# The row transposes of two tensors moved from PE to the DMA queue, and those of two others merged, in a fused forward-and-backward kernel

## The chip, the cores and the metric

The kernel runs on one core of one Trainium2 chip. The metric is the device time of one execution in microseconds (us). The time before was 828.26 us (median of 3 runs, 827.59 to 828.33).

The engines are called as the profile calls them: PE is TensorE (matrix multiply), PEld its weight loads, DVE is VectorE, ACT is ScalarE, POOL is GpSimd, SP is SyncE, which here does nothing but issue DMA transfers. "SPq" is SP's queue.

## The reference, cut to what matters

```python
# x [2,16000,256], w1, w2 [3,256,256], g [2,8,256], w_f, w_g, w_o [256,256], all bf16
h  = gelu(conv(x, w1))[:, ::2]          # 3 taps, stride 2
f  = gelu(conv(h, w2))[:, ::2]          # 3 taps, stride 2: 4000 rows per batch
j  = tanh((f @ w_f)[:, :, None] + (g @ w_g)[:, None])
out = j @ w_o                           # [2,4000,8,256]
# returned: out and the gradients of all seven inputs, for a given grad_out
```

The gradient with respect to `h` is what this case is about. The kernel holds it as two tensors, one for the odd rows of `h` (`GHo`) and one for the even rows (`GHe`), each with the 256 channels on partitions (two halves of 128) and time along the free axis. The gradient of `w1` contracts over time, so it needs the same numbers with time on partitions: their row layouts, `GHoR` and `GHeR`.

## The kernel before

The 4000 rows of each batch are cut into chunks of at most 512, 18 chunks in all: 256, seven of 512, 160; seven of 512, 256, 160. The kernel first records operations with modelled costs. A greedy scheduler (`issue`) then fixes the order of each engine's instructions from those costs. In the trace of before, all 6428 matmuls and all 536 DMA instructions of SP start in that order. While chunk k is in its main part (tanh, `j @ w_o`, backward of both), the backward of chunk k-1 (`stage_de`) and the convolutions of chunk k+1 (`stage_a`) fill the gaps.

The row layouts of `GHo` and `GHe` are made on PE, as a multiplication by the identity into PSUM, and copied to SBUF by ACT or DVE:

```python
    def to_rows(cls, SRC, off, n, keys):
        dst = buf(cls, [P, NB, D], BF16, cls.upper())
        ps = psum(BF16)
        nbl = (n + P - 1) // P

        def trs(e):
            for bl in range(nbl):
                m = min(P, n - bl * P)
                for kt in range(KT):
                    nc.tensor.transpose(out=ps[:m, (bl * KT + kt) * P:(bl * KT + kt + 1) * P],
                                        in_=SRC[:, kt, off + bl * P:off + bl * P + m], identity=ident[:])
        op("PE", c_pe([P] * (nbl * KT)), trs, r=[(SRC, k) for k in keys] + [ident], w=[ps], new=[ps, dst])
        # ... one or two evictions ps -> dst by ACT or DVE, cut
```

The rows of `h` itself (`HRo`, `HRs`, `HRe`) and of `f` (`FR`) already come from transposing DMAs that SP issues, one for each half of the channels:

```python
    def dma_rows(name, cls, g_, SRC, off, keys, nb):
        W = chunks[g_][3]
        Wp = (W + P - 1) // P * P
        R = buf(cls, [P, KT, NB, P], BF16, name)
        st[g_][name] = R
        for kt in range(KT):
            dma("SP", lambda kt=kt: R[:, kt, 0:Wp // P, :], lambda kt=kt: SRC[:, kt, off:off + Wp],
                r=[(SRC, kt)] + [(SRC, k) for k in keys], w=[(R, kt)], bytes_=Wp * P * 2, new=[R] if kt == 0 else [],
                transpose=True, nb=nb)
```

What the scheduler believes about a DMA is in these lines. A transposing DMA keeps SP busy for 1260 ns, and its data is counted as there 2000 ns plus a margin of 6500 ns after the modelled transfer:

```python
        c = 1260.0 if transpose else 400.0 if q == "SP" else cost or (750.0 if q == "POOL" else 100.0)
        return op(q, c, go, r=r, w=w, new=new, at=at, after=after, hold=hold, nb=nb,
                  work=bytes_ / 256 * 1.25 if transpose else bytes_ / 300.0)
    # ... in issue():
                o.done = ring[e] + 2000.0 + self.MARGIN          # MARGIN = 6500.0
```

And this is where the rows are made, in `stage_de`, after the weight gradients of the second convolution. They are used last in the stage, after the `gx` matmuls:

```python
        GHoR = to_rows("rows", GHo, 0, Wsp, [0, 1, "z"])
        tick()
        GHeR = to_rows("rows", GHe, 1, Wsp, [0, 1, "z"])
        tick()
        # ... gx: gradient of x from GHo, GHe, W1T; then the three taps of the gradient of w1:
        #     wgrad(ACC1, i, ..., [(X5 rows, GHoR, ...), (X5 rows, GHeR, ...)], out_2[i])
```

## Time and profile before

| what | before |
|---|---|
| median, 3 runs | 828.26 us |
| span of the profiled run | 826.2 us |
| PE / DVE / ACT busy | 97% / 92% / 91% |
| a full chunk repeats every (first weight load of `JT` to that of the next chunk) | 49.20 us |
| time of SP's DMA instructions, summed | 632 us |

The first part of the page gives each engine's busy time, its share of the span and its instructions:

```profile
PE 798.5 (97%) x6428; PEld 593.9 (72%) x6428; DVE 763.1 (92%) x1731; ACT 749.2 (91%) x1206; POOL 186.6 (23%) x393
```

Three engines above 90% do not say which one bounds the kernel. The table by stretches does. Its columns are the stretch and its length, then busy time (and instructions) of each engine, the granted PE clock, the busy share of the DMA engines and what they moved:

```profile
core 0: us, PE busy (x) PEld busy (x) DVE busy (x) ACT busy (x) POOL busy (x), PEclk, DMA share, GB/s
50.00:100.00 50.00, 47.77 (x353) 32.86 (x351) 49.01 (x109) 49.38 (x80) 12.14 (x24) 1.00 1.05 218
600.00:650.00 50.00, 50.00 (x394) 36.57 (x393) 47.67 (x101) 46.97 (x71) 10.09 (x21) 1.00 0.94 221
```

In mid-kernel PE has no idle time at all, so PE is the limit there. From 50 to 100 us DVE and ACT are nearly as full as they can be, and PE has 2.2 us to spare.

The work that the change takes from PE, and the evictions that go with it, are in the list of groups by form. The columns are the instruction, its operands, their number, then busy time and mean ns of one, then the idle time before them:

```profile
L314 ACT COPY ROWS<-psb 128x1024 bf16<-128x1024 bf16 x42 | 43.5, 1036 | 0.2 <-PE psb L491 0.2
...
L491 PE MATMUL psb<-ident,GHo 128*128 128x128 bf16 x128 | 10.1, 219 | 0.0
L491 PE MATMUL psb<-ident,GHe 128*128 128x128 bf16 x128 | 10.1, 219 | 0.0
```

There are 256 transposes. "219 ns" is the recorded time of one from start to end, not what it costs a full queue: the records overlap, and 253 of the 256 are followed by the next matmul 55 or 56 ns after their start. The `ROWS` evictions here are those of `GHo`, `GHe`, `NGFE` and `GF` together.

The DMA side: the queues that carry the traffic, with packets, MB and the share of the 16 engines' span that the packets took, and two lines of the table of waits (total us, times, longest):

```profile
q1 hardware_dynamic: 314004, 120.54, 70.5%
q0 software_dynamic: 15840, 49.98, 18.6%
```

```profile
DVE g_sq L706 <- DMA out_dram<-g_sq: 9.9, 4, 4.8
...
PE ps L306 <- DMA GOT<-in_grad_out_dram: 2.1, 1, 2.1
```

The packets of these two queues fill 89% of the DMA engines' time, yet PE waited for a load only once after the weights of the start. The waits of DVE on the stores of `g_sq` are in the tail, where the weight gradients are written out through two buffers.

### The profile page before, as it was taken

To read this page: it belongs to the slowest core of one execution; us is meant where nothing else is said; L and a number is where in the kernel's file an instruction comes from. 1 tells how busy PE (TensorE), PEld (TensorE's weight loads), DVE (VectorE), ACT (ScalarE), POOL (GpSimd) and SP (SyncE) were. 2 spreads that over 40 slices of the span, in tenths; PEclk is the share of its full clock that TensorE was granted. 3 is DMA by queue.
4 is the path that set the end of the run, shared out by engine and by line. 5 is a ranking of instruction groups with operands and counts; after the bars stand their busy time and mean duration, and the time that the engine had idled before them with its cause. 6 is when DMAs were issued, how large, how long until landed. Compare 5 with 4: busy or idle time off the path is not lost.

```text
span 826.2 us, 18042 instructions
## 1 busy us (share of the span) xinstructions
PE 798.5 (97%) x6428; PEld 593.9 (72%) x6428; DVE 763.1 (92%) x1731; ACT 749.2 (91%) x1206; POOL 186.6 (23%) x393
## 2 busy tenths in 40 slices
PE   7789999999999999999999999999999999999994
PEld 5556677686777868787877677686767768788983
DVE  4999999998989999998979999999989999998982
ACT  6999999999898989998899999999998989998752
POOL 3111203122221212232222122122111212213241
PEclk9999999999999999999999999999999999999998
DMA  8979999999899896968799999989899897957442
GB/s 185 238 158 233 220 195 275 239 246 267 190 249 216 205 239 173 250 185 215 163 213 243 221 203 248 202 218 241 192 255 187 225 224 192 245 163 188 122 137 68
DMA packets 330718, 172.06 MB, mean 208 GB/s; under 512 B 275236, under 2 KB 310344, under 8 KB 330628
## 3 DMA queue, kind: packets, MB, share of 16 engines
q1 hardware_dynamic: 314004, 120.54, 70.5%
q0 software_dynamic: 15840, 49.98, 18.6%
q8 instruction: 50, 0.82, 0.5%
q10 hardware_dynamic: 784, 0.39, 0.2%
q14 instruction: 40, 0.33, 0.1%
HBM read 54.44 MB, written 50.34 MB: 127 GB/s over the span
## 4 chain that ended last, share of the span: by engine, by line
PE 75%; DVE 10%; ACT 9%; DMA 3%; issue 2%; DVEq 0%; POOL 0%; ACTq 0%
PE ps L306 61%; PE GWO L306 11%; PE psb L491 4%; DVE NGZ L659 2%; DVE ZS L667 2%; ACT JT L597 2%; ACT g_sq L440 1%; ACT JR L617 1%; ACT JSQ L649 1%; DVE g_s L444 1%; DMA GOT<-in_grad_out_dram 1%; ACT OUT_SB L314 1%; ACT GX_SB L316 1%; DMA XC<-in_x_dram 1%; DMA W<-in_w_dram 1%
## 5 line engine op out<-in xcount | busy, mean ns | idle before, releaser
L597 ACT ACTIVATE JT<-FE,GE 128x512 bf16<-128x512 bf16 (+2 forms) x288 | 188.0, 690 | 0.7 <-DVE FE L319 0.7
L331 POOL DMA_DIRECT2D out_dram<-OUT_SB x136 | 94.9, 698 | 383.6 <-ACT OUT_SB L314 275.0
L659 DVE SCALAR_TENSOR_TENSOR NGZ<-JSQ,ps 128x512 f32<-128x512 bf16 (+2 forms) x252 | 155.0, 618 | 2.3 <-PE ps L306 2.2
L306 PE MATMUL ps<-GOT,WT 128*128 128x512 bf16 (+2 forms) x576 | 153.3, 351 | 2.4 <-DMA GOT<-in_grad_out_dram 2.1
L306 PE MATMUL ps<-WO,JT 128*128 128x256 bf16 x1024 | 154.0, 273 | 1.6 <-ACT JT L597 1.0
L617 ACT ACTIVATE JR<-JR 128x1024 bf16<-128x1024 bf16 x128 | 138.3, 1086 | 4.9 <-DVE JR L610 4.6
L306 PEld LDWEIGHTS <-JT 128*128 128x128 bf16 x1024 | 99.6, 98 | 54.8 <-ACT JT L597 1.8
L314 ACT CAST OUT_SB<-ps 128x512 bf16<-128x512 f32 x205 | 125.9, 615 | 9.5 <-PE ps L306 9.5
L306 PE MATMUL GWO<-GO_R,JR 128*128 128x256 bf16 x1024 | 132.7, 273 | 1.2 <-ACT JR L617 1.2
L667 DVE TENSOR_TENSOR ZS<-ZS,NGZ 128x512 f32<-128x512 f32 (+2 forms) x216 | 133.6, 622 | 0.2
L649 ACT ACTIVATE JSQ<-JT 128x1024 bf16<-128x1024 bf16 (+2 forms) x119 | 117.6, 991 | 12.0 <-DVE NGZ L659 11.9
L306 PEld LDWEIGHTS <-JR 128*128 128x128 bf16 x1028 | 99.9, 98 | 19.4 <-ACT JR L617 2.9
L306 PEld LDWEIGHTS <-WT 128*128 128x128 bf16 x864 | 81.3, 98 | 38.0 <-DMA GOT<-in_grad_out_dram 2.3
L306 PEld LDWEIGHTS <-W 128*128 128x128 bf16 x648 | 61.2, 98 | 56.6 <-DMA W<-in_w_dram 2.8
L306 PE MATMUL ps<-XC,W 128*128 128x512 bf16 (+2 forms) x432 | 92.2, 351 | 0.8 <-DVE NGZ L659 0.8
L306 PE MATMUL ps<-ROWS,X 128*128 128x256 bf16 x768 | 92.0, 273 | 0.0
L610 DVE TENSOR_TENSOR JR<-FER,GEB 128x1024 bf16<-128x1024 bf16 x128 | 88.8, 696 | 1.1 <-PE GWO L306 1.0
L306 PEld LDWEIGHTS <-X 128*128 128x128 bf16 x768 | 75.1, 98 | 9.1
L444 DVE SCALAR_TENSOR_TENSOR g_s<-g_sq,ps 128x512 bf16<-128x512 bf16 (+2 forms) x108 | 66.4, 616 | 14.7 <-ACT HTo L442 11.8
L715 DVE TENSOR_TENSOR ACC<-ACC,ps 128x512 f32<-128x512 f32 x96 | 65.1, 690 | 11.4 <-PE ps L306 11.3
L306 PE MATMUL ps<-WT,GHe 128*128 128x256 bf16 x384 | 73.3, 273 | 0.7 <-ACT ROWS L314 0.7
L306 PE MATMUL ps<-WT,GHo 128*128 128x256 bf16 x384 | 73.1, 273 | 0.7 <-ACT GX_SB L316 0.7
(135 smaller groups left out, 1262.3 us busy)
## 6 DMA issues: line engine op xcount, KB each, us to landing
GO_R<-in_grad_out_dram SPq DMA_DIRECT2D x120, 256.0 KB, 3.9
out_dram<-OUT_SB POOLq DMA_DIRECT2D x120, 256.0 KB, 4.2
X<-in_x_dram SPq DMA_DIRECT2D x60, 320.0 KB, 5.8
out_dram<-GX_SB POOLq DMA_DIRECT2D x60, 256.0 KB, 3.9
GOT<-in_grad_out_dram SPq DMA_TRANSPOSE x144, 3.8
out_dram<-g_sq SPq DMA_DIRECT2D x9, 128.0 KB, 1.9
GO_R<-in_grad_out_dram SPq DMA_DIRECT2D x8, 128.0 KB, 2.7
out_dram<-OUT_SB POOLq DMA_DIRECT2D x8, 128.0 KB, 3.7
```

What stands on the lines that cost most here:

```text
L306: nc.tensor.matmul(ps_ap, lhsT=lhsT, rhs=rhs, start=start, stop=stop)
L314: nc.scalar.copy(out=dst(), in_=src())
L331: return eng_.dma_start(out=out(), in_=in_())
L444: op("DVE", c_dve(W), lambda e, mt=mt, ps=ps: nc.vector.scalar_tensor_tensor(out=s[:, mt, :W], in0=sq[:, mt, :W], scalar=1.0, in1=ps[:, :W ...
L491: nc.tensor.transpose(out=ps[:m, (bl * KT + kt) * P:(bl * KT + kt + 1) * P], in_=SRC[:, kt, off + bl * P:off + bl * P + m], identity=ident[:])
L597: op("ACT", c_act(W, ptr=True), lambda e, j=j, mt=mt: nc.scalar.activation(out=JT[:, j, mt, :W], in_=S["FE"][:, mt, :W], func=ACT.Tanh, bi ...
L610: op("DVE", c_dve(n * 2 * D, 0.5), lambda e, lo=lo, n=n, m=m, JR=JR: nc.vector.tensor_tensor(out=JR[:m, lo % 2:lo % 2 + n], in0=S["FER"][: ...
L617: op("ACT", c_act(n * 2 * D), lambda e, lo=lo, n=n, m=m, JR=JR: nc.scalar.activation(out=JR[:m, lo % 2:lo % 2 + n], in_=JR[:m, lo % 2:lo % ...
L649: nc.scalar.activation(out=JSQ[:, :, :W], in_=JT[:, j, :, :W], func=ACT.Square)
L659: op("DVE", c_dve(W) + 6, lambda e, d2=d2, ps=ps, u=u, zap=zap, JSQ=JSQ: nc.vector.scalar_tensor_tensor(out=zap(), in0=JSQ[:, d2, :W], sca ...
L667: op("DVE", c_dve(W), lambda e, d2=d2, dst=dst, NGZ=NGZ: nc.vector.tensor_tensor(out=dst[:, d2, :W], in0=ZS[:, d2, :W], in1=NGZ[:, :W], op ...
L715: op("DVE", c_dve(512), lambda e: nc.vector.tensor_tensor(out=acc_ap().rearrange("p k d -> p (k d)"), in0=acc_ap().rearrange("p k d -> p ( ...
```

## The change

The intent: take 256 matmuls and half of the `ROWS` evictions off the compute engines by making `GHoR` and `GHeR` with SBUF-to-SBUF transposing DMAs; and, to make room in SP's queue, transpose both halves of the channels in one DMA where the source has no padding columns (`HRe` and `FR` in the 14 full chunks). The core of the diff (the adaptation of the row views in `wgrad` is cut):

```diff
-    def dma_rows(name, cls, g_, SRC, off, keys, nb):
-        W = chunks[g_][3]
-        Wp = (W + P - 1) // P * P
-        R = buf(cls, [P, KT, NB, P], BF16, name)
+    def dma_rows(name, cls, g_, SRC, off, keys, nb=None, at=None):
+
+        n = (chunks[g_][3] + off_extra.get(name, 0) * (chunks[g_][1] == last_ci[chunks[g_][0]]) + P - 1) // P
+        R = buf(cls, [P, KT * NB * P], BF16, name)
 ...
+        if SRC.shape[-1] == n * P:
+            dma("SP", lambda: R[:].rearrange("p (g q) -> p g q", q=P), lambda: SRC[:].rearrange("p k w -> p (k w)"),
+                r=[(SRC, k) for k in [0, 1] + keys], w=[R], bytes_=KT * n * P * P * 2, new=[R], transpose=True, nb=nb, at=at)
+            return R
         for kt in range(KT):
 ...
-        GHoR = to_rows("rows", GHo, 0, Wsp, [0, 1, "z"])
+        GHoR = dma_rows("GHoR", "rows", g_, GHo, 0, ["z"])
         tick()
-        GHeR = to_rows("rows", GHe, 1, Wsp, [0, 1, "z"])
+        GHeR = dma_rows("GHeR", "rows", g_, GHe, 1, ["z"])
```

Note that the merge does not reach the new transposes: `GHo` and `GHe` are 514 columns wide, so `GHoR` and `GHeR` go out as two DMAs each, four a chunk.

More of the change, by code (lines that the diff above doesn't have):

```diff
@@ L253 @@
         start_of.append(start_of[-1] + c[3])
+    off_extra = {"GHoR": 1, "GHeR": 1}
+    last_ci = {c[0]: c[1] for c in chunks}
     nblk = [[(tb, P) for tb in range((W + P - 1) // P)] for (_, _, _, W) in chunks]
@@ L464, in conv_gelu @@
         return go
-    def dma_rows(name, cls, g_, SRC, off, keys, nb):
-        W = chunks[g_][3]
-        Wp = (W + P - 1) // P * P
-        R = buf(cls, [P, KT, NB, P], BF16, name)
+    def dma_rows(name, cls, g_, SRC, off, keys, nb=None, at=None):
+        n = (chunks[g_][3] + off_extra.get(name, 0) * (chunks[g_][1] == last_ci[chunks[g_][0]]) + P - 1) // P
+        R = buf(cls, [P, KT * NB * P], BF16, name)
+        view = lambda: R[:, 0:KT * n * P].rearrange("p (k b q) -> p k b q", k=KT, q=P)
+        R.rows = lambda m, bl: view()[:m, :, bl, :]
+        R.cols = lambda m, bl, d2: view()[:m, d2, bl, :]
         st[g_][name] = R
+        if SRC.shape[-1] == n * P:
+            dma("SP", lambda: R[:].rearrange("p (g q) -> p g q", q=P), lambda: SRC[:].rearrange("p k w -> p (k w)"),
+                r=[(SRC, k) for k in [0, 1] + keys], w=[R], bytes_=KT * n * P * P * 2, new=[R], transpose=True, nb=nb, at=at)
+            return R
         for kt in range(KT):
-            dma("SP", lambda kt=kt: R[:, kt, 0:Wp // P, :], lambda kt=kt: SRC[:, kt, off:off + Wp],
-                r=[(SRC, kt)] + [(SRC, k) for k in keys], w=[(R, kt)], bytes_=Wp * P * 2, new=[R] if kt == 0 else [],
-                transpose=True, nb=nb)
+            dma("SP", lambda kt=kt: view()[:, kt], lambda kt=kt: SRC[:, kt, off:off + n * P],
+                r=[(SRC, k) for k in [kt] + keys], w=[(R, kt)], bytes_=n * P * P * 2, new=[R] if kt == 0 else [],
+                transpose=True, nb=nb, at=at)
+        return R
     def pad_tail(g_, SRC, off):
@@ L483, in to_rows @@
         dst = buf(cls, [P, NB, D], BF16, cls.upper())
+        dst.rows = lambda m, bl: dst[:m, bl, :]
         ps = psum(BF16)
@@ L807, in mms @@
                 for k, (lhs, rhs, bl, m, d2) in enumerate(jobs):
-                    mm(ps[:, d2 * D:(d2 + 1) * D], lhs(bl, m, d2), rhs[:m, bl, :], k == 0, k == len(jobs) - 1)
+                    r_ = rhs.rows(m, bl)
+                    o_ = ps[:, d2 * D:(d2 + 1) * D]
+                    mm(o_ if len(r_.shape) == 2 else o_.rearrange("p (k q) -> p k q", k=KT), lhs(bl, m, d2), r_, k == 0, k == len(jobs) - 1)
             rd = [rhs for _, rhs, _, _ in pairs]
@@ L815, in rows_lhs @@
         def rows_lhs(T_):
-            return lambda bl, m, d2: T_[:m, d2, bl, :]
+            return lambda bl, m, d2: T_.cols(m, bl, d2)
         wgrad(ACCF, 0, lambda: ACCF[:], [(rows_lhs(S["FR"]), NFR, nblk[g_], [S["FR"]])], out_5)
```

## The prediction

> **What bounds the kernel now.** TensorE (PE). The profile page shows PE busy 97% of the 826.2 us span, DVE 92%, ACT 91%. The table of 50 us stretches has PE busy 49.5 to 50.0 of every 50 us from 100 to 800, at clock 1.00. From 75 to 800 us successive matmuls start at the gap of their size (216 ns for 512 columns, 109 for 256, 56 for 128); the excess adds up to about 4 us. So there a matmul that disappears is worth its issue interval, whatever other engines do. Only the first 60 us (loads) and the tail after 802 us (small dependent steps, nine stores through two buffers) are bound otherwise.
>
> **What it removes.** PE transposes of GHo and GHe and their evictions. The groups of instructions list 128 transposes of each. "Busy" charges them 20.2 us (79 ns each)[...]; in a full queue they start 56 ns apart: 256 x 56 ns = 14.3 us. [...] Half of the ROWS evictions go too: about 26 us of ACT (1036 ns per 128x1024) and 5 us of DVE; both had slack, so I count nothing.
>
> **What it adds.** 72 SBUF-to-SBUF DMA transposes (four a chunk), 32,768 packets of 256 B. Such packets took 18 ns at the median, 23.6 on average: 37 to 48 us of the 16 engines. All packets fill 90% of the span now, at their median durations about 68%; I expect a share near 0.96 and longer landings (4 to 5 us), no new limit. SP issues a transpose in about 1.25 us: +91 us. Merging HRe and FR in the 14 full chunks removes 28 issues: -35 us, if a merged one issues as fast (GOT, with twice an HR half's bytes, does: 1264 ns). SP's DMA instructions go from about 632 us to 690 of 812.
>
> **Why this stays hidden.** In the table of waits PE waits 2.1 us in all on GOT, and on no other load after the weights. GOT has eight buffers, a whole chunk ahead; the rows of GHo and GHe are needed only after the gx matmuls.
>
> **The tail.** There the new transposes are exposed: four issues (5 us) and 2.3 us of landing after the last GHe (807 us now) stand in SP's queue ahead of eight stores, and in the new order 24 weight-gradient matmuls of the chunk before last move behind the last NGFE matmuls. Much hides behind the gx evictions, which last until 814 us. I allow 0 to +3 us.
>
> **Sum.** 828.3 - 14.3 + about 1 = 815 us (-1.6%). Range 810.5 to 822. Faster by over 2%: 0.12. Within 2%: 0.83. Slower by over 2%: 0.05.
>
> **What would show each step right or wrong.** Right: PE still busy 49.5 of 50 us from 100 to 780; a full chunk repeats about 0.9 us (16 x 56 ns) sooner than the 49.2 us in the chain of waits now; ACT busy about 26 us less; transposes left on PE only for FE, NGFE and GF; DMA share up by about 0.06. Wrong: PE waiting over 1 us in mid-kernel for GOT, GO_R, XC, HRe, GHoR or GHeR; merged transposes issuing in 2.5 us; a tail over 3 us longer.
>
> **What would make it wrong.** SP, which issues in order, blocking on GHo or GHe while loads behind it fall due; the order of work, recomputed by the kernel's scheduler, opening new PE gaps[...].

## The result, and the profile after

The change runs in 819.67 us (median of 4 runs, 818.28 to 819.90); the kernel before, in the same rounds, in 827.92 (4 runs, 827.25 to 828.33). The ratio is 0.9898, with a 95% interval of 0.988 to 0.9915. Here and below a ratio is the mean time of one kernel's fast runs over that of the other's of the same rounds, so not quite the ratio of the medians quoted beside it. It is a gain of 1.0%, where 1.6% was predicted: 4.7 us of the expected 13 are missing.

The page of the profiled run (span 818.0 us):

```profile
PE 783.7 (96%) x6081; PEld 580.9 (71%) x6172; DVE 751.7 (92%) x1712; ACT 729.6 (89%) x1189; POOL 188.0 (23%) x393
```

PE's count is 6081 where 6172 weight loads are recorded, so 91 matmul records are missing from this trace. PE's busy time is therefore not comparable, and start times of weight loads are used below. ACT is 19.6 us and DVE 11.4 us less busy: 31 in sum, as predicted (26 and 5), but split otherwise, since the scheduler gave ACT more of the other evictions.

The same two stretches as before:

```profile
core 0: us, PE busy (x) PEld busy (x) DVE busy (x) ACT busy (x) POOL busy (x), PEclk, DMA share, GB/s
50.00:100.00 50.00, 41.99 (x290) 28.56 (x294) 42.47 (x93) 42.55 (x66) 9.57 (x18) 0.93 1.08 219
600.00:650.00 50.00, 49.63 (x377) 36.32 (x382) 47.46 (x99) 46.68 (x73) 10.11 (x20) 1.00 1.06 235
```

Mid-kernel looks as predicted (49.63 with five records missing). From 50 to 100 us something new happened: PE is 5.8 us less busy, DVE 6.5 and ACT 6.8, and the clock is 0.93. The table of waits names it:

```profile
PE ps L308 <- DMA GHoR<-GHo: 4.1, 1, 4.1
...
DVE g_sq L717 <- DMA out_dram<-g_sq: 3.8, 6, 1.0
...
PE ps L308 <- DMA GHeR<-GHe: 0.8, 1, 0.8
```

Each new wait occurs once. PE's timeline shows when (columns: start, us, instruction, number; in brackets the idle time before and what ended it). The first line is the last work before the stop, the others are the first uses of the rows of chunk 0:

```profile
87.63 1.04 PE L308 MATMUL GWO<-GO_R,JR 128*128 128x256 bf16 x8
92.79 0.58 PE L308 MATMUL ps<-GHoR,X 128*128 128x256 bf16 x2 [4.13 <-DMA GHoR<-GHo]
94.19 0.61 PE L308 MATMUL ps<-GHeR,X 128*128 128x256 bf16 x2 [0.81 <-DMA GHeR<-GHe]
94.59 0.63 PE L308 MATMUL ps<-GHoR,X 128*128 128x256 bf16 x2
```

PE stands still from 88.5 us (the last of eight matmuls, which start 109 ns apart from 87.63, starts at 88.39, so the next would have started there; the 1.04 us run to the recorded end of the last, 88.66) to 92.79, 4.3 us. Then a pair of matmuls starts 0.40 us after the pair before it; at full clock a matmul of 256 columns starts every 109 ns, a pair every 0.22. The clock was halved, as the table of stretches of 2 us shows (the clock is the number before the last two; the first line is of before, the others of the change):

```profile
92.00:94.00 2.00, 2.00 (x18) 1.49 (x17) 2.00 (x5) 2.00 (x5) 0.00 (x0) 1.00 1.10 334
...
90.00:92.00 2.00, 0.00 (x0) 0.00 (x0) 0.16 (x1) 2.00 (x3) 0.00 (x0) 0.73 1.08 215
92.00:94.00 2.00, 0.58 (x2) 0.14 (x2) 0.00 (x0) 0.00 (x1) 0.00 (x0) 0.50 0.96 276
94.00:96.00 2.00, 1.81 (x9) 1.29 (x10) 0.32 (x1) 0.00 (x0) 0.00 (x0) 0.50 1.13 266
96.00:98.00 2.00, 2.00 (x13) 1.40 (x12) 0.98 (x3) 0.00 (x0) 0.00 (x0) 0.57 0.99 210
```

The half clock lasted from 90.9 to 97.7 us, 6.8 us. It began 2.4 us after the stop of 4.3 us had begun, while PE still stood. The last section gathers what the traces show of the half clock.

Why did the rows come late? `GHo` of chunk 0 was complete at 62.1 us and `GHe` at 65.5 (ends of the DVE instructions that write them). This is SP's queue after that; the second column is how long SP was occupied:

```profile
63.65 6.70 SPq L331 DMA_TRANSPOSE XC<-in_x_dram  x2
...
72.42 1.17 SPq L331 DMA_TRANSPOSE GHoR<-GHo  x1
73.68 0.53 SPq L333 DMA_DIRECT2D GO_R<-in_grad_out_dram  x1
74.27 2.58 SPq L331 DMA_TRANSPOSE HRo<-HTo  x2
76.89 2.58 SPq L331 DMA_TRANSPOSE HRs<-HTo  x2
...
83.76 3.06 SPq L331 DMA_TRANSPOSE GOT<-in_grad_out_dram  x2
86.91 1.78 SPq L331 DMA_TRANSPOSE GHoR<-GHo  x1
88.74 2.55 SPq L331 DMA_TRANSPOSE GHeR<-GHe  x2
```

Before, SP was no faster in the same place:

```profile
63.56 7.74 SPq L329 DMA_TRANSPOSE XC<-in_x_dram  x2
```

The data was there; SP was not. The first half of `GHoR` went out at 72.4 us, the second at 86.9, the last half of `GHeR` at 90.1, which is 24.6 us after `GHe` was complete. For the next chunks this delay is 10.5, 10.9, 7.2, 5.0 and 3.4 us. So SP's queue runs late at the start of the kernel, and catches up. (Around the short chunk in the middle the delay rises once more, to 12.8 us for chunk 8, half of that of chunk 0, and no wait follows.)

It did so before the change too. The last of the transposes for chunk k (`FR`) was issued this long after the start of chunk k-1, in us:

| kernel | k=1 | 2 | 3 | 4 | 5 |
|---|---|---|---|---|---|
| before | 64.5 | 58.2 | 56.2 | 50.5 | 46.7 |
| after | 59.1 | 52.1 | 44.3 | 46.7 | 42.7 |

In the steady part it is about 46 us (before) and 43 (after). So the kernel before was 18, 12 and 10 us late for k = 1, 2 and 3 (for k = 1 a part of it is only that chunk 0 is half as long), and this cost nothing, since the rows of `h` and `f` there were issued at least 12 us before their first use. In the change, PE had come to the rows of chunk 0 at 88.5 us, 23.0 us after `GHe` was complete, which is 1.6 us before the last issue. In the next chunks the first use comes 5.9, 8.7, 12.0 and 14.2 us after the last issue.

Where the 8.2 us between the two profiled spans came from, by the first weight load of `JT` in each chunk:

| part | after minus before, us |
|---|---|
| until chunk 0 begins | +1.65 |
| chunk 0 | -1.15 |
| chunk 1 (backward of chunk 0) | +8.50 |
| chunks 2 to 16 | -14.56 |
| from the start of chunk 17 to the end | -2.60 |
| sum | -8.16 |

The +1.65 us at the start look like chance and not like an effect of the change. In the change's trace the clock was halved from 12.4 to 15.8 us, before the first chunk. Of the 14 traces seven have such a stretch, and chunk 0 begins at 21.9 to 22.6 us in them; seven have none (before and e2, but also e1, e3, e4, e6 and e12, described below, which hold all or most of the change), and it begins at 20.7 to 21.5.

A full chunk now repeats every 48.31 us instead of 49.20: 0.89 us, where 16 transposes x 56 ns are 0.90. All 232 transposes in chunks 2 to 16 make 13.0 us, so nearly the whole gain of those chunks is theirs. The +8.5 us of chunk 1 is 4.9 us of waits as the profile counts them, and about 1.75 us for the half clock (3.5 us of matmuls between 94.2 and 97.7 that would have taken half); the rest is refilling of the other engines, which were idle too (argued, not measured).

The DMA queue, as predicted (0.96 for all queues; it is 0.98):

```profile
q1 hardware_dynamic: 348180, 128.94, 77.9%
q0 software_dynamic: 15840, 49.98, 19.2%
```

There are exactly 32,768 more packets of 256 B than before, at a median of 18 ns, and SP's DMA instructions now sum to 689 us (predicted 690). The 14 merged `HRe` issue in 1.25 us at the median, the 14 merged `FR` in 1.45 (1.23 to 3.59); one half of `FR` took 1.22 in before. So merging saves issue time. It does not follow that size is free: an `XC` transpose occupies SP for 2.85 us at the median of the whole run, not only at the start (before 3.01), where the scheduler counts 1.26.

### The profile page after: what moved, and what is told of

It is laid out like the page before. It is cut to its first block, busy times and chain, and to the rows that moved or that the text cites. A ratio compares the mean times of both kernels' runs of the same rounds, so it can differ in the third digit from the quotient of the medians.

```text
span 818.0 us, 17507 instructions
## 1 busy us (share of the span) xinstructions
PE 783.7 (96%) x6081; PEld 580.9 (71%) x6172; DVE 751.7 (92%) x1712; ACT 729.6 (89%) x1189; POOL 188.0 (23%) x393
## 4 chain that ended last, share of the span: by engine, by line
PE 66%; DVE 14%; ACT 13%; DMA 3%; issue 3%; ACTq 0%; DVEq 0%; POOL 0%
PE ps L308 55%; PE GWO L308 9%; ACT JT L608 3%; DVE NGZ L670 3%; DVE ZS L678 2%; PE psb L502 2%; ACT JSQ L660 2%; ACT OUT_SB L316 2%; ACT JR L628 2%; DVE g_s L446 1%; DVE JR L621 1%; ACT g_sq L442 1%; DVE OUT_SB L321 1%; DMA out_dram<-OUT_SB 1%; ACT g_s L452 1%
## 5 line engine op out<-in xcount | busy, mean ns | idle before, releaser
L608 ACT ACTIVATE JT<-FE,GE 128x512 bf16<-128x512 bf16 (+2 forms) x288 | 186.0, 682 | 0.7 <-DVE FE L321 0.7
L628 ACT ACTIVATE JR<-JR 128x1024 bf16<-128x1024 bf16 x128 | 137.6, 1077 | 11.4 <-DVE JR L621 10.8
L308 PE MATMUL ps<-GOT,WT 128*128 128x512 bf16 (+2 forms) x522 | 141.3, 348 | 0.7
L660 ACT ACTIVATE JSQ<-JT 128x1024 bf16<-128x1024 bf16 (+2 forms) x115 | 111.7, 973 | 11.9 <-DVE NGZ L670 11.7
L308 PEld LDWEIGHTS <-JR 128*128 128x128 bf16 x1028 | 100.0, 98 | 20.7 <-ACT JR L628 3.2
L442 ACT ACTIVATE g_sq<-ps 128x512 bf16<-128x512 f32 (+2 forms) x108 | 59.6, 552 | 14.8 <-PE ps L308 12.8
```

What stands on the lines that cost most here:

```text
L308: nc.tensor.matmul(ps_ap, lhsT=lhsT, rhs=rhs, start=start, stop=stop)
L442: op("ACT", c_act(W, True), lambda e, mt=mt, ps=ps: nc.scalar.activation(out=sq[:, mt, :W], in_=ps[:, :W], func=ACT.Square, scale=GELU_SQR ...
L608: op("ACT", c_act(W, ptr=True), lambda e, j=j, mt=mt: nc.scalar.activation(out=JT[:, j, mt, :W], in_=S["FE"][:, mt, :W], func=ACT.Tanh, bi ...
L628: op("ACT", c_act(n * 2 * D), lambda e, lo=lo, n=n, m=m, JR=JR: nc.scalar.activation(out=JR[:m, lo % 2:lo % 2 + n], in_=JR[:m, lo % 2:lo % ...
L660: nc.scalar.activation(out=JSQ[:, :, :W], in_=JT[:, j, :, :W], func=ACT.Square)
```

## The experiments

All give correct results unless said. "Chunk 1" is the time from the start of chunk 1 to that of chunk 2 in the profiled run, 43.38 us in before and 51.88 in the change.

### First call: whose fault is the stall?

Theory A: only the rows of the first chunk are late, because the loads of the start are in SP's way. Theory B: the DMA traffic or the order of work as a whole makes the chunk slow. Neither fits what follows. The reading that does was A2: SP's queue is late for several chunks, and the first rows that are needed before it has caught up make PE wait, whichever they are.

**e1: rows of chunk 0 on PE, the rest by DMA.**

```diff
-        GHoR = dma_rows("GHoR", "rows", g_, GHo, 0, ["z"])
+        by_pe = g_ == 0
+        GHoR = to_rows("rows", GHo, 0, Wsp, [0, 1, "z"]) if by_pe else dma_rows("GHoR", "rows", g_, GHo, 0, ["z"])
# and the same for GHeR
```

> The change, but the rows of GHo and GHe of the first chunk alone are made by TensorE again. Theory A (the only loss is that the first chunk's GHoR and GHeR are issued late in the SP queue, TensorE reaches the matmuls that read them and stands still, 5.9 us, and then works 6.8 us at half clock): the second chunk's period goes from 51.9 back to 43 to 44 us, the time to 811 to 812 us. Theory B (the chunk is slow because of the DMA traffic or the order of work as a whole, with merged transposes and HR loads): the period stays above 49 us, the time at 818 or more.

Measured: 820.39 us (820.26 to 827.06; before 828.31, 827.49 to 829.85), ratio 0.9923 (0.9884 to 0.9962). Chunk 1 is back at 43.37 us, but chunk 2 takes 56.65 instead of 47.71. PE's timeline has the first use of the rows of chunk 1:

```profile
130.09 1.01 PE L308 MATMUL ps<-GHoR,X 128*128 128x256 bf16 x4 [5.19 <-DMA GHoR<-GHo]
133.33 1.04 PE L308 MATMUL ps<-GHeR,X 128*128 128x256 bf16 x4 [2.23 <-DMA GHeR<-GHe]
```

The stall has moved by one chunk and has grown. Theory A falls: without the stall in chunk 1 the queue is still late one chunk later (the last `GHeR` of chunk 1 goes out 19.0 us after its data, 10.5 in the change). Theory B falls too, since chunk 1 is back, though the time is the one that B expected.

**e2: merged DMAs for `HRe` and `FR` only; all rows of `GHo` and `GHe` on PE.**

```diff
-        GHoR = dma_rows("GHoR", "rows", g_, GHo, 0, ["z"])
+        by_pe = True          # with the choice of e1
```

> Only the merged transposes of HRe and FR, GHo and GHe on TensorE as before. Theory A: nothing on TensorE changes, so the full chunks keep 49.2 us and the time stays within 1.5 us of before (828); SP's issues fall by about 35 us. A rival, that the steady gain of 0.89 us a chunk comes from the shorter SP queue and not from the missing transposes: the period falls below 48.8 us.

Measured: 828.27 us (826.85 to 829.14), ratio 0.9997 (0.9982 to 1.0012). SP's DMA instructions fell from 632 to 597 us, and a full chunk still repeats every 49.20 us. The merge alone gains nothing: the gain in the steady part is that of the removed PE transposes.

**e3: the change without the merge.**

```diff
-        if SRC.shape[-1] == n * P:
+        if False and SRC.shape[-1] == n * P:
```

> The rows of GHo and GHe by DMA, HRe and FR not merged: 28 more SP issues. Theory A: full chunks keep 48.3 us, since SP has slack there; the stall in the second chunk grows by the two additional issues ahead of GHeR, 1 to 3 us; 820 to 823 us. If merging were needed to make room in the SP queue, full chunks would take over 48.8 us and the time would be over 826.

Measured: 831.14 us (829.49 to 832.52), ratio 1.0039 (1.0021 to 1.0057). A miss for the expected time: it is slower than the kernel before. SP's instructions sum to 739 us. Chunk 1 takes 59.28 us, and waits for the new rows come back later, five times for `GHeR`:

```profile
PE ps L308 <- DMA GHoR<-GHo: 7.8, 1, 7.8
PE ps L308 <- DMA GHeR<-GHe: 6.7, 5, 2.3
```

Full chunks without a stall still repeat every 48.31 us. So the merge, worth nothing alone, is what the new transposes need: 28 issues fewer are 11 us here (831.1 against 819.7). They were run at other times.

**e4: the first use of the rows of chunk 0 put later, by about 80 matmuls.**

```diff
-    ..., GHeR, sblk, [])], out_2[i])
+    ..., GHeR, sblk, [])], out_2[i], t0 + dt * 1.25 if g_ == 0 else None)   # priority time of the matmuls
```

> The change with all its DMAs in the same order up to the first chunk's GHeR; only the 24 matmuls that read the first chunk's GHoR and GHeR stand some 80 matmuls (about 10 us) later in TensorE's order. Theory A: they find their data, no wait on GHoR or GHeR over 1 us, no half clock after 90 us, second chunk near 43 us plus or minus the moved 2.6 us, time 810 to 813. Theory B (traffic or the engines' order as a whole): the second chunk stays slow, 817 or more.

Measured: 822.86 us (819.13 to 827.27), ratio 0.9935 (0.9894 to 0.9976). Chunk 1 takes 42.81 us, with no stall; the 24 matmuls (2.6 us) now run in chunk 2. But chunk 2 takes 62.70 (47.71 before), with PE waiting for `GHoR` of chunk 1, so the expected 810 to 813 us are missed:

```profile
137.46 1.01 PE L308 MATMUL ps<-GHoR,X 128*128 128x256 bf16 x4 [9.88 <-DMA GHoR<-GHo]
```

This agrees with e1 and says more. A stall stops PE while SP goes on, so the stall itself lets SP catch up. Taken away in chunk 1, the lateness stays in the queue (25.1 us for the last `GHeR` of chunk 1, 10.5 in the change), and the next consumer pays, more. A longer lead for one consumer is no cure.

### Second call: the lateness, and cures

**e5: the scheduler told that an `XC` transpose occupies SP for 3300 ns instead of 1260.** In the change's queue above, two of them took 6.70 us.

```diff
-        c = 1260.0 if transpose else 400.0 if q == "SP" else ...
+        c = (cost or 1260.0) if transpose else 400.0 if q == "SP" else ...
 # load_xc: dma(..., transpose=True, at=at, cost=3300.0)
```

> Nothing is moved between engines; only the scheduler's cost of issuing one XC transpose is set to 3.3 us, what the trace shows, in place of 1.26. Theory A2 (in the first chunks the SP queue runs behind the order that the scheduler believed in, by up to 18 us; the change reads its new rows so soon after their issue that the lag becomes a stall of TensorE): the order now allows for it, the stall in the first three chunks shrinks below 2 us, time 810 to 814. Theory B2 (the DMA engines, not the order, limit the first chunks: as many bytes must pass before the first GHeR lands): the stall stays 5 us or more, 817 or more.

Measured: 816.94 us (815.74 to 817.90; before 828.01, 826.76 to 828.85), ratio 0.9865 (0.985 to 0.988). The wait for `GHoR` is gone, 2.3 us for `GHeR` are left, and chunk 1 takes 44.44 us. A new order brings a new wait, though: 3.9 us of PE on ACT, up to 49.5 us, and the half clock for 3.4 us after it. The corrected cost gets back more than half of what was missing, less than expected. That it does so by making SP less late is not shown: the order as a whole is new, and the last `GHeR` of chunk 0 still goes out 25.0 us after its data.

**e6: rows of chunks 0 to 3 on PE, the rest by DMA.**

```diff
-        GHoR = dma_rows("GHoR", "rows", g_, GHo, 0, ["z"])
+        by_pe = g_ < 4        # with the choice of e1
```

> The change, but GHo and GHe of the first four chunks are turned on TensorE. In the run of before the SP queue has caught up with its steady place in the chunk by the fifth chunk. Theory A2: no stall anywhere, first five chunks at the periods of before, then 48.3 us; 12 us under before less nothing, 813 to 815.5. Theory A1 (the first chunk that is turned by DMA always stalls): a stall of 5 us or more moves to the sixth chunk, 819 or more.

Measured: 816.25 us (814.38 to 816.84), ratio 0.9854 (0.9838 to 0.9869). It beats both kernels. The same stretches, and its first line of the page:

```profile
PE 790.5 (97%) x6228; PEld 584.2 (72%) x6228; DVE 753.5 (93%) x1716; ACT 733.4 (90%) x1193; POOL 188.2 (23%) x393
```

```profile
50.00:100.00 50.00, 47.77 (x354) 33.01 (x353) 48.89 (x108) 49.38 (x80) 12.03 (x24) 1.00 1.08 231
600.00:650.00 50.00, 50.00 (x380) 35.96 (x378) 47.46 (x99) 46.67 (x72) 11.79 (x24) 1.00 1.10 234
```

There is no wait on `GHoR` or `GHeR` in the table of waits at all, and the idle column of their matmuls is zero:

```profile
L308 PE MATMUL ps<-GHeR,X 128*128 128x256 bf16 x300 | 46.5, 273 | 0.0
L308 PE MATMUL ps<-GHoR,X 128*128 128x256 bf16 x300 | 46.5, 273 | 0.0
```

It keeps 56 transposes on PE (28 of each tensor), so it removes 200, or 200 x 56 ns = 11.2 us: from 828.0 that is 816.8, and 816.25 was measured (0.75 us above the range for e6). Here the arithmetic of the prediction closes, if not term by term: in the profiled run the part from chunk 17 on is 2.5 us shorter than before, and only 0.9 of it are transposes. Theory A2 stands: by chunk 4 the queue has caught up (the last `GHeR` of chunk 4 goes out 5.7 us after its data are ready, against 24.6 for chunk 0 in the change).

**e7: plain loads (`GO_R`, `X`) issued by POOL instead of SP,** to leave SP to the transposes.

```diff
-LOADQ, STOREQ = "SP", "POOL"
+LOADQ, STOREQ = "POOL", "POOL"
```

> The change with its 206 plain loads (GO_R and X) issued by GpSimd in place of SP: same bytes, same transposes, about 105 us less for the SP queue. Theory A2: GHoR and GHeR of the first chunks are issued early, TensorE waits for them less than 1 us; if the loads behind GpSimd's waiting stores come in time, 810 to 813; if not, TensorE waits for GO_R or X, which would be a fault of this experiment and not of the theory. Theory B2 (bytes): the wait on GHoR and GHeR stays 5 us or more.

Measured: 872.55 us (854.26 to 903.04). Three of the four runs count as slow, the profiled one (span 901.3 us, clock 0.952) among them, so there is no ratio and the sizes are not used. A miss all the same: even the fastest run is 26 us slower than before. In the profile, of a slow run, PE waits for the rows in many chunks (and once each for `GO_R`, 8.4 us, and `GOT`, 6.7 us):

```profile
PE ps L308 <- DMA GHeR<-GHe: 38.0, 7, 9.5
PE ps L308 <- DMA GHoR<-GHo: 17.1, 4, 8.5
```

Issue time is not small in the change, where SP's DMA instructions take 689 of 818 us. Even so the other issuer brought no gain: the issues of `GOT` alone grew from 215 to 296 us in total on SP, though SP had fewer DMAs to issue. What slowed them stays open, the more as the run was slow. The edit also does more than change the issuer: the bytes are the same, but the loads moved in packets of 4096 and 5120 bytes, where SP's had used 1024 and 2560.

### Third call: bytes or issues, and how far it can be taken

Is SP late because the transfers are slow (bytes), or because it has too many to issue? e3 showed that the number of issues matters. e10 changes the bytes (and, with them, a third of the store packets).

**e10: the stores of the largest output cut to half their bytes,** with the same instructions in the same order on PE and SP. Half of that output is not written, so the result is wrong.

```diff
-   dst_[0:nb * P].rearrange("(a p) n -> p a n", p=P),        OUT[:, 0:nb]....
+   dst_[0:nb * P].rearrange("(a p) n -> p a n", p=P)[:, :, 0:V],  OUT[:, 0:nb]....[:, :, 0:V]
```

> Wrong on purpose: the changed kernel, with the stores of out_0 writing half of the columns (16.4 MB less of about 180); the orders of TensorE and of the SP queue are those of the change, instruction by instruction. Theory B3 (the SP queue lags in the first chunks because its transfers share 16 full DMA engines with the stores): with 9% fewer bytes XC and GOT issues pass faster, GHoR and GHeR of the first chunk land in time, waits on them under 2 us, 809 to 813. Theory A3 (the lag is issue time of SP alone, not bytes): the first issue of GHeR stays within 1 us of 88.7 to 90, the stall stays 4 us or more, 817 or more.

Measured: 816.23 us (814.10 to 819.66; before 828.42, 826.84 to 830.91), ratio 0.9851 (0.9822 to 0.988). Chunk 1 takes 47.09 us (51.88 in the change, 43.38 before); PE waits 1.7 us for `GHoR` and 0.4 for `GHeR` (4.1 and 0.8 in the change), the clock stays at 1.00, and the two `XC` take 5.83 us on SP instead of 6.70. That is 4.8 us less than in the change, about half of its loss in chunk 1 (and still 2.7 us less than in e14 below, where the change itself was profiled again and did better than the first time). The delay of the last `GHeR` is still 22.6 us. Both theories miss their time. So both count: with fewer bytes in flight the same issues take less time (SP's DMA instructions sum to 656 us; 684 to 689 in the change, e13 and e14), and with fewer issues (e3 against the change) SP is less late.

**e11: e6, with `GHo` stored without its two padding columns, so that its two halves are merged from chunk 4 on.**

```diff
-        GHo = buf("gho", [P, KT, CW + 2], BF16, "GHo")
+        GHo = buf("gho", [P, KT, CW], BF16, "GHo")        # and by_pe = g_ < 4
```

> The version with the first four chunks on TensorE, and GHo allocated 512 columns wide, so that its two halves too are turned by one DMA in full chunks (10 fewer SP issues). Both theories: no stall, full chunks at 48.3 us; within 1 us of the version without it, 814 to 816.5; faster than that only if short waits on SP are left somewhere.

Measured: 817.28 us (817.06 to 818.22), ratio 0.9862 (0.9844 to 0.9879), not separable from e6 in ratio. The chunks before 17 are as in e6. With no wait left to remove, fewer issues gain nothing, as in e2. From chunk 17 on, e11 takes 42.69 us where e6 takes 40.50: in its order DVE waits 6.1 us for the final stores, 3.8 in e6.

**e12: e11, and the rows of a third tensor (`NGFE`) by one merged DMA in full chunks from chunk 5 on.**

```diff
-        NFR = to_rows("rows", NGFE, 0, Wp, [0, 1, "z"])
+        NFR = dma_rows("NFR", "rows", g_, NGFE, 0, ["z"]) if g_ >= 5 and W == CW else to_rows("rows", NGFE, 0, Wp, [0, 1, "z"])
```

> As the run before, and the rows of NGFE too by one merged DMA in the full chunks from the sixth on: 8 transposes fewer on TensorE in each of 10 chunks, 256 KB more for the DMA engines each. If the engines and SP have room: 10 x 0.45 us = 4.5 us less, 810 to 812.5. If the DMA engines are full by now, TensorE waits on NFR, GHoR or GHeR in mid-kernel and the time is above the run before.

Measured: 814.43 us (813.32 to 818.16), ratio 0.9832 (0.9806 to 0.9858), the fastest median of all, but the intervals of e6, e11 and e12 overlap. A full chunk repeats every 48.10 us, 0.21 less than in the change, where 8 transposes x 56 ns would be 0.45, and the expected 810 to 812.5 us are missed. A merged `NFR` occupies SP for 2.57 us at the median (1.23 to 3.58), and new short waits appear around chunk 9:

```profile
447.64 0.39 PE L308 MATMUL ps<-GHoR,X 128*128 128x256 bf16 x2 [0.97 <-DMA GHoR<-GHo]
449.13 0.38 PE L308 MATMUL ps<-GHeR,X 128*128 128x256 bf16 x2 [1.09 <-DMA GHeR<-GHe]
```

The half clock followed here too, from 450.2 to 453.6 us. This path is near its end.

### Fourth call: the half clock by itself, and the change again

**e13: 44 useless matmuls ahead of the first use of `GHoR`, to keep PE busy through the wait.** Their result is overwritten. If the half clock is a loss of its own, this should gain.

```diff
             def mms(e):
+                if g_ == 0 and ACC is ACC1 and key == 0:
+                    for _ in range(44):
+                        mm(ps[:, 0:D], ident[:], W2[:, 0, 0], True, True)
                 for k, (lhs, rhs, bl, m, d2) in enumerate(jobs):
```

> The changed kernel, with 44 matmuls of 256 columns without use (4.8 us at full clock, overwritten by what follows) in front of the first matmul that waits for the first chunk's GHoR; every other instruction in its order. If the half clock after the stall (6.8 us from 91 to 98 us in the trace) is a cost of its own, caused by the idle time, then work without use in the idle time removes it: no stretch at half clock between 85 and 110 us, second chunk 49 to 50.5 us in place of 51.9, about 2 us less than the change run beside it. If it is not, the second chunk stays at 51.5 or more (or gains as many us as the filler takes too long).

**e14: the change again,** unaltered, as the partner of e13.

> The changed kernel itself again, to be compared with the run of this call and to see how far its stall varies: 818.5 to 820.5, second chunk 50 to 54 us, stall on GHoR and GHeR 5 to 8 us.

Measured: e13 818.76 us (818.18 to 824.65), ratio 0.9885 (0.9868 to 0.9902); e14 820.91 (817.67 to 824.64), ratio 0.9919 (0.9894 to 0.9945); before 827.65 (826.68 to 830.40). The two intervals overlap, so no gain is shown. In e13's profile (one of its two slowest runs) SP was later than in the change's, chunk 1 took 54.43 us, PE still waited 2.9 us for `GHoR`, and the clock was halved for 3.4 us all the same. The experiment is inconclusive; what the half clock costs by itself remains the estimate above (about 1.75 us).

e14 showed something else. The same kernel was profiled with chunk 1 at 49.83 us instead of 51.88 and a wait of 3.4 us instead of 4.1, and its runs spread over 7 us, those of before over 4. How long the stall is varies from run to run.

## Why the prediction was right or wrong

- **What bounds the kernel: right.** PE without idle time in mid-kernel made every removed transpose worth its issue interval. The chunk shortened by 0.89 us for 16 transposes, 56 ns each, which is also the gap between their start times in the trace of before. e6 closes the sum: 200 x 56 ns expected, 828.0 to 816.25 measured.
- **What it adds: right.** 32,768 packets of 256 B, a DMA share of 0.98 for 0.96, SP at 689 us for 690, merged transposes issuing in 1.25 (`HRe`) and 1.45 us (`FR`), not 2.5. `GOT` now lands 4.4 us after issue (3.8 before), within the 4 to 5 us expected.
- **What it removes on ACT and DVE: right in sum** (31 us), wrong in the split; it bounds nothing.
- **"Why this stays hidden": the step that failed.** The prediction argued from waits that the kernel before showed, and from the place of the new rows in the program ("needed only after the gx matmuls"). That PE waited for no load before did not mean that SP was on time. SP was late by 10 to 18 us in the first chunks, and no wait showed it, since the rows that it then issued had 12 us or more to spare. The new rows had none: the last of chunk 0 went out 24.6 us after its data were ready, and PE wanted it after 23.0. In the change's profiled run that made 4.9 us of waits, then 6.8 us of half clock, and 8.5 us in chunk 1 instead of a gain. The prediction named the mechanism among the things that could go wrong ("SP, which issues in order"; PE waiting for `GHoR` or `GHeR`), but gave it no microseconds and looked for it in mid-kernel, not at the start.
- **The tail: wrong in sign.** 0 to +3 us were allowed; it became 2.6 us shorter, of which 0.9 are removed transposes. In before, DVE waits 9.9 us for the nine final stores, which pass through two buffers; after, 3.8 us, in the table of waits. In the new order these stores follow each other evenly. That the order makes the difference was not tested by itself, but the runs point to it: e2 (merge only) has the long tail of before, 42.7 us from chunk 17 on, and so has e11, which has no transposes of `GHo` and `GHe` on PE there.
- **The sum.** 256 x 56 ns is 14.3 us. Add about 9 us for the stall (8.5, and the 0.45 us that the eight transposes of chunk 0 should have saved there), subtract 1.7 for the tail; the remaining -1 us is spread over the start (+1.65, by chance as it seems) and the catching up. It comes to the -8.2 us of the two profiled spans. The predicted 815 us was the time without the stall. That the measured 819.67 lies inside the range of 810.5 to 822 is owed to the width of the range, and to a shorter tail that nobody foresaw; the stall had no term in the sum.

What stays open: the weight of the half clock by itself, what sets the time for which an `XC` transpose occupies SP (1.4 to 5.4 us in the change), and why SP's issues grew longer when the plain loads went to POOL.

## What to carry to other kernels

Where PE had no idle time, a removed transpose was worth its issue interval of 56 ns (0.89 us a chunk for 16), and that was predicted to the tenth of a microsecond; whether the work that replaces it stays hidden is a question of lead time, chunk by chunk. Before giving a queue a new consumer, read from the trace how late that queue runs, above all in the first chunks: "nobody waits for it" may only mean that everybody so far had time. If the queue is late at the start, keep the old path for the first chunks and switch when it has caught up (e6: no wait left); lengthening one consumer's lead only handed the wait to the next here (e4: 9.88 us).

## What these traces show of the queue, the packets and the clock

- Queue lag on the issuing engine: here it was 24.6 us from data ready to last issue in chunk 0, 3.4 us for chunk 5 and 12.8 for chunk 8. In this kernel SP's DMA instructions took 689 of 818 us.
- SP issue time of a transposing DMA under load: the runs show medians of 1.22 us for one half of `FR` (before), 1.45 for both halves in one (the change), and 2.85 for an `XC` transpose (the change).
- Packets: in the change's trace a 256-byte packet, as the transposes are made of, takes 18 ns at the median, and one of 4096 bytes 161 ns. As an estimate, 16 engines at those medians move 228 and 407 GB/s. Packet size alone may account for the difference (an estimate from this trace): packets of 512 and 1024 bytes, which are not transposes, take 27 and 46 ns, and a straight line through these two gives about 18 ns at 256 bytes.
- The half clock: in the change's trace the granted clock changes at 12.40, 15.81, 90.91, 97.73 and 814.53 us, and the times between are 1, 22, 2 and 210 times 3.41 us. In the 3.41 us before the three falls to half, PE was busy, as the profile counts it, for 0.92, 1.17 (from 87.5 to 90.9) and 0.00 us. In the other such stretches at full clock, after which it stayed, PE was busy for 2.02 us or more; in before's trace it was 0.04 us ahead of the one fall and 1.82 or more elsewhere. How long PE stands still does not decide it alone: in e12 PE waited 0.97 and 1.09 us for `GHoR` and `GHeR` of one chunk, 1.46 us busy in the 3.41 before the fall at 450.2; in e10 it waited 1.70 and 0.38 us, and the clock stayed at 1.00. What decides it was not tested.
